# A fused attention, slot-mixture and feed-forward kernel: another buffer for the first head pair's maxima, and later places for the second and third pair's preparation

## The chip, the cores and the metric

The kernel runs on one core of one Trainium2 chip. The metric is the device time of one execution in microseconds (us), taken as the median of several runs.

## The reference, cut to what matters

Three stages follow one another. The change touches the first one alone.

```python
# attention: q, k, v are (4, 8, 1152, 64)
q_pool = q.reshape(B, H, S // 2, 2, D).mean(axis=3)      # 576 pooled queries
scores = matmul(q_pool, k.T) / sqrt(D)                    # 576 x 1152 for each head
attn = exp(scores - max(scores, axis=-1)); attn /= sum(attn) + 1e-9
out = matmul(attn, v)
# then a mixture with 8 experts x 4 slots (softmax over tokens and over slots)
# then x @ w_in, a piecewise quadratic activation, @ w_out
```

## The kernel before, in words

The 32 heads are handled as 16 pairs, P = 0 to 15. The keys of a pair are split into a high and a low fp16 part, which lie side by side in `kn` (`prep_khi` on ScalarE, L265; `prep_klo` on VectorE, L273, or on GpSimd for P = 1, L271), and are transposed by DMA into `K1[P]` (`xpose_k`, L279), one half of the tile for each head. The queries of a pair are added up in twos (`prep_qp`, L286), rounded to fp16 (`prep_qhi`, L289 and L291), transposed by DMA (`xpose_q1`, L301), and their remainder is kept in `qn2` (`prep_qlo`, L296). For P > 1 one more DMA copies the upper half of `q1[P]` into its lower half (`dup_q1`, L304). All loads, transposes and copies are issued by SyncE (SP), one after another.

A pair then has two jobs on TensorE. **Its maxima**: for each of nine query tiles t, `max_half(P, t, 0)` multiplies the queries by the difference of two halves of the keys (`KD`, written by `k_diff`, L315), ScalarE takes the positive part into `RW[:, t % 2]` (L332); `max_half(P, t, 1)` multiplies the queries by the first half, and VectorE adds and takes the running maximum (L335). `RW` has two places. The PSUM results take a tile of the pool `sc`, which has three buffers of two banks; two more banks, `acc0` and `acc1`, are the accumulators of the output. `max_fin(P)` turns the nine maxima into a row of the second query matrix `q2[P]`; for P = 0 this is done by TensorE (L354) and three evictions (L358 to L360), between two runs of filling products of the identity with itself (`fill`, L344). For P = 0 each `max_half(0, t, 0)` also issues two filling products (L330). **Its scores and output**: for each of nine key tiles c and each head h, `st` makes the scores (L383) and their exponential on ScalarE (L388, into a tile `e`), `pv` multiplies them by the values one step later (L408), and `es_add` sums the exponentials on VectorE (L394).

The order of the work is written out by hand. The steps are g = -11 to 144, two slots (h = 0, 1) in each; step g = 9 P + c does `st(P, c, h)`, `pv` of step g - 1, and the maxima of the pair that comes about one pair later. The first pair's maxima are at g = -11 to -3 with nothing beside them. The second pair's are at the steps that `P1G` lists, the third pair's start at g = 7. In a slot the order of issue is: maxima, `st`, `pv`, then what `sched` has for this slot, in the order in which `at` was called: `R1` (the second pair's preparation), the `k_diff` calls, and then pair by pair what `plan(P)` adds. `plan` turns a number x of `PREP` or `KDS` into the slot x % 2 of step 9 P + x // 2. Every engine and SP take their instructions in this order.

For P > 1 the loads go to buffers of which there is one: `kf` for keys, `qf` for queries, `kn` for the split keys. The pool hands a buffer to the next pair's tile only when everything that reads the tile before it is done, also a reader that stands later in the order; the engine that writes the new tile waits for it.

Of the kernel before, what the change touches and what calls it, by code (L numbers as in the profile page):

```python
# [12 lines left out]
AF = mybir.ActivationFunctionType  # L13
# [4 lines left out]


WARM = 8, 0, 4, 2, 6, 3, 3, 2  # L20
FILL = 38, 1, 6, 5

MB = {1: 3, 2: 10, 3: 20}
DU = (3, 4, 5)

CVS = (10, 12, 17, 18, 19), (8, 9, 10, 11, 12)
CVL = 1
P1G = 0, 1, 1, 2, 2, 3, 4, 5, 6
TML = (3, 0, 4), (6, 1, 4)
WPH = 6  # L30

# [2 lines left out]
       tuple((2 * c + h + 1 + (c < 8), c, h) for c in range(1, 9) for h in range(2)))  # L34
ADD += tuple((16, *x[1:]) if x == (17, 7, 0) else x for x in ADD[0]),

PREP = (-20, (-36, -35), (-34, -33), (-33, -32), -33, -32, -31, -30), (-24, (-42, -40), (-37, -37), (-35, -34), -38, -37, -35, -31)
KDS = -26, -19


@with_exitstack
def fused_kernel(ctx: ExitStack, tc: tile.TileContext, q, k, v, phi, w1, w2, w_in, w_out, out):
    nc = tc.nc
# [6 lines left out]
    HQ = TQ // 2  # L50
# [21 lines left out]
    def sc_tile(name):  # L72
        return sc_p.tile([128, 2, 512], F32, tag="sc", name=name)
# [95 lines left out]
    RW = g2.tile([128, 2, 2, HQ], F32, name="RW")  # L169
# [59 lines left out]
    K1, q1, q2, vt, qft, kft, qpt, mp = {}, {}, {}, {}, {}, {}, {}, {}  # L229
# [6 lines left out]
    def load_k(P, h):  # L236
        b, hp = divmod(P, HPB)
        if h == 0:

            kft[P] = g0.tile([128, 2, NK, D], F32, tag="kf", name=f"kf{P}") if P != 1 else \  # L240
                xT[:, 0:2].rearrange("p h (c d) -> p h c d", c=NK)
        nc.sync.dma_start(out=kft[P][:, h], in_=k[b, 2 * hp + h].rearrange("(p c) d -> p c d", p=128))
# [67 lines left out]
    def key_half(P, h):  # L310
        return K1[P][:, h * NK:(h + 1) * NK, :].rearrange("p c k -> p (c k)")
# [5 lines left out]
    def max_half(P, t, a):  # L317
        if t == 0 and a == 0:
            mp[P] = g2.tile([128, NK], F32, tag="mp", name=f"mp{P}")
        ps = sc_tile(f"mx{P}_{t}_{a}")  # L320
        parts = [(0, 64, 0 if t <= 4 else 1), (64, 128, 0 if t < 4 else 1)]
        for i in range(2):
            for (p0, p1, h) in parts:
                kk = key_half(P, h) if a else KD[:, h]
                nc.tensor.matmul(ps[p0:p1, i, 0:HQ], lhsT=q1[P][:, t, p0:p1], rhs=kk[:, i * HQ:(i + 1) * HQ],  # L325
                                 start=True, stop=True)
        if P == 0 and a == 0:
            for _ in range(FILL[1]):
                for p0 in (0, 64):
                    nc.tensor.matmul(fl[0][p0:p0 + 64, 0:HQ], lhsT=q1[P][:, t, p0:p0 + 64], rhs=kk[:, 0:HQ], start=True, stop=True)  # L330
        if a == 0:
            nc.scalar.activation(out=RW[:, t % 2], in_=ps[:, :, 0:HQ], func=AF.Relu)  # L332
        else:
            r = RW[:, t % 2]
            nc.vector.tensor_tensor_reduce(out=r, in0=ps[:, :, 0:HQ], in1=r, scale=1.0, scalar=-3.0e38, op0=ALU.add, op1=ALU.max,  # L335
                                           accum_out=mp[P][:, t:t + 1])

    fl = {}

    def fill(n):  # L340
        if not fl:
            fl[0] = acc_tile(0, "fill")
        for _ in range(n):
            nc.tensor.matmul(fl[0][:, 0:128], lhsT=ident, rhs=ident, start=True, stop=True)  # L344

    def max_fin(P):
        qn2 = qn2b[P % 2]
        nc.vector.tensor_scalar(out=qn2[:, :, D], in0=mp[P], scalar1=-1.0 / MS, scalar2=None, op0=ALU.mult)
        if P == 0:
            fill(FILL[2])  # L350
            ps = sc_tile("mr")
            po = [ps[64:96, 0], ps[64:96, 1], acc_tile(1, "mr8")[64:96]]
            for t in range(NK):
                nc.tensor.matmul(po[t // 4][:, t % 4 * 128:t % 4 * 128 + 128], lhsT=qn2[:, t, D:D + 1].to_broadcast([128, 32]),  # L354
                                 rhs=identh, start=True, stop=True)
            fill(FILL[3])
            f2 = q2[P].rearrange("p c k -> p (c k)")[64:96]
            nc.scalar.activation(out=f2[:, 0:512], in_=po[0], func=AF.Copy)  # L358
            nc.vector.tensor_copy(f2[:, 512:1024], po[1])
            nc.vector.tensor_copy(f2[:, 1024:1152], po[2][:, 0:128])  # L360
        else:
            xpose_q2(P)

    def xpose_q2(P):
        q2[P] = pr_p[P % 2].tile([128, NK, 128], F16, tag="q2", name=f"q2_{P}")
        nc.sync.dma_start_transpose(out=q2[P], in_=qn2b[P % 2].rearrange("p c k -> p (c k)"))
# [3 lines left out]
    def acc_tile(i, name):  # L370
        return acc_p.tile([128, 512], F32, tag=f"acc{i}", name=name)
# [192 lines left out]
    def at(g, slot, f, *a):  # L564
        sched.setdefault((g, slot), []).append((f, a))

    def plan(P):
        b = NK * P
        if P > 1:
            lk, hk, lok, xk, aq, hq_, xq, loq = PREP[P > 2]  # L570

            def sl(x, f, *a):
                at(b + x // 2, x % 2, f, *a)

            for h in range(2):
                at(b + lk, h, (load_k2, load_q)[h], P)
                sl(hk[h], prep_khi, P, h)
                sl(lok[h], prep_klo, P, h)
                sl(xk[h], xpose_k, P, h)
                sl(KDS[h], k_diff, P, h)  # L580
            sl(aq, prep_qp, P)
            sl(hq_, prep_qhi, P)
            sl(xq, xpose_q1, P)
            sl(loq, prep_qlo, P)
            sl(xq + (6 if P > 2 else 4), dup_q1, P)
        if P > 0:
            at(b - 8, 1, load_v, P)
            at(b - 4, 0, s2_fill, P, 0, 5)
            at(b, 0, s2_fill, P, 5, NK)
        last = P == NP - 1  # L590
        for s, *a in ADD[2 if P in (5, 9, 13) else last]:
            at(b + s // 2, s % 2, es_add, P, *a)
        if not last:
            pre.setdefault((b + 9, 0), []).append((es_sum, P))
        q_ = P // HPB
        if last:
            at(b + 9, 0, t_raw, P, 0)
            at(b + 9, 1, t_raw, P, 1)
            for f, *a in ((es_sum, P), (t_sum, P, 0), (t_sum, P, 1), (t_fin, P), (t_x, P, True), (warm, WARM[0]), (t_last, P),
                          (lg_mx, q_), (lg_tr, q_), (warm, WARM[5]), (lg_max, q_), (lg_rep, q_), (p_old, q_), (warm, WARM[1]), (lg_exp, q_),  # L600
                          (p_mm, q_), (warm, WARM[6]), (p_add, q_)):
                at(b + 10, 0, f, *a)
            return
        g0 = b + (11 if P == NP - 2 else 18)
        pre.setdefault((g0, 0), []).insert(0, (t_x, P))
        for i in range(2):
            at(g0, 0, t_ev, P, i)
        at(b + 10, 0, t_fin, P)
        for c, h, t in TML:
            at(g0 + c // 2, c % 2, t_mul, P, h, t)  # L610
        at(g0 + 3, 1, lg_add, P)
        for h in range(2):
            at(b + 9, h, t_raw, P, h)
            at(b + 9, h, t_sum, P, h)
        if P % HPB == HPB - 1:
            for s, f, *a in ((10, lg_mx), (12, lg_tr), (12, lg_max), (14, lg_rep), (14, lg_exp), (16, p_mm), (16, p_add)):
                late.setdefault((g0 + s // 2, s % 2), []).append((f, (q_, *a)))

    def slot(g, i):
        for d in (sched, late):  # L620
# [2 lines left out]

    R1 = (((-10, 1), (prep_khi, 1, 0), (prep_klo, 1, 0), (xpose_k, 1, 0)),
          ((-8, 1), (prep_khi, 1, 1), (prep_klo, 1, 1), (prep_qp, 1)),
          ((-6, 1), (xpose_k, 1, 1)),
          ((-3, 0), (prep_qhi, 1), (xpose_q1, 1)))

    with tc.manual_schedule():
        load_k(0, 0)  # L630
# [3 lines left out]
        load_k(1, 1)  # L634
        fill(FILL[0])
        nc.vector.memset(S2[64:128], 0.0)
# [31 lines left out]
                at(g, i, *x)  # L668
        at(-9, 1, k_diff, 0, 1)
        at(-3, 1, k_diff, 1, 0)  # L670
        at(0, 0, k_diff, 1, 1)
        at(1, 1, prep_qlo, 1)
        at(CVL, 1, cv_load, 0)

# [6 lines left out]
        for P in range(NP):  # L681
            plan(P)
# [11 lines left out]
        for g in range(-LEAD, nsteps + 1):  # L694
            mx = [divmod(g + LEAD, NK)] if not NK <= g + LEAD < 2 * NK else []
            mx += [(1, t) for t in range(NK) if P1G[t] == g]
            P, c = divmod(g, NK)
# [53 lines left out]
        def over_slots(ps, src):  # L751
            for dc in range(4):
                nc.tensor.matmul(ps[:, dc * NS:(dc + 1) * NS], lhsT=src[:, dc * 128:(dc + 1) * 128], rhs=st4,
                                 start=True, stop=True)
            return ps[:, 0:4 * NS].rearrange("p (c k) -> p c k", c=4)

        ps = over_slots(sc_tile("sT")[:, 0, :], Prun)
# [429 lines left out]
```

## Time and profile before

| | |
|---|---|
| median of 3 runs | 702.65 us (702.56, 702.65, 704.59) |
| the profiled execution's own time | 703.25 us |
| its span, first to last instruction | 701.4 us |
| busy: TensorE, VectorE, ScalarE, GpSimd | 690.0, 556.4, 497.5, 139.4 us |
[...]
| attention, g = -11 to 144 | from 12.3 us to about 430 us |

The times in the views below count from the start of the span. A row of the timeline gives the start, the duration, the engine, the line, the operation, written and read tiles, shape, count, and in brackets how long the engine had been idle and what ended that. PE is TensorE, PEld its weight loads, DVE VectorE, ACT ScalarE, SPq the queue of DMAs that SP issues. A matmul's duration runs to its modelled end, so two matmuls that follow one another overlap in the rows; the distance of their starts is what one costs.

### The profile page before, as it was taken

How to read it: one execution, taken by the hardware profiler on the slowest of the kernel's cores; microseconds unless marked ns; L12 is line 12 of the kernel's file. 1: busy time of each engine (PE TensorE's matmuls, PEld its weight loads, DVE VectorE, ACT ScalarE, POOL GpSimd, SP SyncE). 2: the span in 40 equal slices, each digit the busy share in tenths (PEclk: the TensorE clock that was granted, in tenths of full speed). 3: DMA queues.
4: the chain of work that ended last, by engine and by line, in shares of the span. 5: the costliest groups of instructions: out<-in, count | busy, mean ns of one | idle time of the engine just before them, and what ended most of it. 6: DMA issues, size and time to landing. Idle time of an engine off the chain costs nothing.

```text
span 701.4 us, 18916 instructions
## 1 busy us (share of the span) xinstructions
PE 690.0 (98%) x7639; PEld 548.1 (78%) x7639; DVE 556.4 (79%) x1094; ACT 497.5 (71%) x884; POOL 139.4 (20%) x123
## 2 busy tenths in 40 slices
PE   8899999999999999999999999999999999999997
PEld 8678878887888887888887876348888888888886
DVE  5699999999899999999998867327678888796542
ACT  4688888788788887788886865118787686677640
POOL 5100110110110110110010020113444353345340
PEclk9999999999999999999999999999999999999999
DMA  9978789988888987987885567993002212200222
GB/s 210 232 159 217 166 214 232 229 174 237 206 171 243 228 165 215 227 173 212 227 202 162 166 220 279 413 383 111 1 31 91 71 50 76 77 30 1 90 90 91
DMA packets 133766, 118.70 MB, mean 169 GB/s; under 512 B 81392, under 2 KB 103920, under 8 KB 131632
## 3 DMA queue, kind: packets, MB, share of 16 engines
q1 hardware_dynamic: 133680, 117.50, 61.9%
q8 instruction: 60, 0.98, 0.6%
q14 instruction: 26, 0.21, 0.1%
HBM read 82.90 MB, written 8.91 MB: 131 GB/s over the span
## 4 chain that ended last, share of the span: by engine, by line
PE 91%; DVE 4%; DMA 2%; ACT 1%; issue 1%; SPq 0%; POOL 0%; DVEq 0%; POOLq 0%; ACTq 0%
PE po L1023 27%; PE st L383 20%; PE acc L408 19%; PE mx L325 10%; PE h L953 2%; PE acc L401 2%; PE h L766 2%; DVE RW L335 2%; PE fill L344 2%; PE ty L448 1%; DMA Wst<-cv_dr 1%; PE tx L442 1%; PE s2o L823 1%; PE pb L537 1%; DVE es L394 0%
## 5 line engine op out<-in xcount | busy, mean ns | idle before, releaser
L388 ACT ACTIVATE e<-st 128x576 f32<-128x576 f32 x288 | 187.5, 652 | 53.0 <-PE st L383 51.9
L408 PE MATMUL acc<-e,vf 128*64 128x288 f32 x1152 | 198.4, 406 | 0.2 <-ACT e L388 0.2
L394 DVE TENSOR_TENSOR es<-es,e 128x576 f32<-128x576 f32 x194 | 144.4, 758 | 5.7 <-ACT e L388 0.4
L383 PE MATMUL st<-q,K 128*64 128x288 f16 x1152 | 129.5, 287 | 2.0 <-ACT e L388 0.5
L383 PE MATMUL st<-q,S 128*64 128x288 f16 x1152 | 129.5, 286 | 0.0
L335 DVE CUSTOM_DVE_ANT_0 RW<-mx,RW 128x576 f32<-128x576 f32 x144 | 108.4, 755 | 23.8 <-ACT e L388 14.2
L325 PEld LDWEIGHTS <-q 128*64 128x64 f16 x1152 | 74.3, 110 | 55.6 <-issue 8.4
L1023 PE MATMUL po<-whi,ghi 128*128 128x512 f32 x280 | 109.3, 390 | 0.0
L1023 PE MATMUL po<-wlo,ghi 128*128 128x512 f32 x280 | 109.0, 389 | 0.0
L1023 PE MATMUL po<-whi,glo 128*128 128x512 f32 x280 | 108.6, 388 | 0.0
L992 POOL TENSOR_TENSOR glo<-r,ghi 128x1024 fp32r<-128x1024 f32 x34 | 81.9, 2408 | 112.6 <-DVE r L980 66.3
L332 ACT ACTIVATE RW<-mx 128x576 f32<-128x576 f32 x144 | 93.4, 650 | 14.2 <-PE mx L325 9.5
L408 PEld LDWEIGHTS acc<-e,vf 128*64 128x64 f32 x1152 | 84.2, 137 | 2.1 <-ACT e L388 1.2
L383 PEld LDWEIGHTS <-K 128*64 128x64 f16 x1152 | 75.8, 109 | 11.7 <-issue 7.8
L489 POOL TENSOR_TENSOR xl<-xl,ss 128x320 f32<-128x320 f32 x15 | 12.5, 830 | 363.3 <-DVE wst L214 192.4
L383 PEld LDWEIGHTS <-S 128*64 128x64 f16 x1152 | 76.3, 110 | 1.0
L1035 DVE TENSOR_TENSOR pa<-po,pa 128x512 f32<-128x512 f32 (+1 forms) x54 | 36.8, 682 | 38.5 <-PE po L1023 38.4
L325 PE MATMUL mx<-KD,q 128*64 128x288 f16 x576 | 62.4, 287 | 3.1 <-DMA q<-qn 1.4
L325 PE MATMUL mx<-K,q 128*64 128x288 f16 x576 | 62.7, 288 | 0.1
L1023 PEld LDWEIGHTS po<-whi,glo 128*128 128x128 f32 x280 | 52.6, 188 | 11.4 <-POOL glo L992 0.3
L1023 PEld LDWEIGHTS po<-whi,ghi 128*128 128x128 f32 x280 | 52.7, 188 | 10.4 <-issue 0.4
L1023 PEld LDWEIGHTS po<-wlo,ghi 128*128 128x128 f32 x280 | 52.7, 188 | 9.5
(205 smaller groups left out, 900.6 us busy)
## 6 DMA issues: line engine op xcount, KB each, us to landing
w<-in_moe_w_dram SPq DMA_DIRECT2D x76, 256.0 KB, 4.0
w<-in_moe_w_dram SPq DMA_DIRECT2D x12, 1024.0 KB, 10.8
vf<-in_v_dram SPq DMA_DIRECT2D x16, 576.0 KB, 5.9
kf<-in_k_dram SPq DMA_DIRECT2D x30, 288.0 KB, 6.9
f<-in_moe_w_in_dram SPq DMA_DIRECT2D x16, 512.0 KB, 5.2
f<-in_moe_w_out_dram SPq DMA_DIRECT2D x16, 512.0 KB, 3.5
qf<-in_q_dram SPq DMA_DIRECT2D x30, 256.0 KB, 7.7
out_dram<-pa SPq DMA_DIRECT2D x17, 256.0 KB, 2.0
```

The costliest lines, as they stand in the source:

```text
L325: nc.tensor.matmul(ps[p0:p1, i, 0:HQ], lhsT=q1[P][:, t, p0:p1], rhs=kk[:, i * HQ:(i + 1) * HQ], start=True, stop=True)
L332: nc.scalar.activation(out=RW[:, t % 2], in_=ps[:, :, 0:HQ], func=AF.Relu)
L335: nc.vector.tensor_tensor_reduce(out=r, in0=ps[:, :, 0:HQ], in1=r, scale=1.0, scalar=-3.0e38, op0=ALU.add, op1=ALU.max, accum_out=mp[P][:, ...
L344: nc.tensor.matmul(fl[0][:, 0:128], lhsT=ident, rhs=ident, start=True, stop=True)
L383: nc.tensor.matmul(ps[c0:c0 + 64, i, 0:HQ], lhsT=kk[:, ci, c0:c0 + 64], rhs=f[:, sl[i]], start=first, stop=not first)
L388: nc.scalar.activation(out=e, in_=ps[:, :, 0:HQ], func=AF.Exp, scale=ESC)
L394: nc.vector.tensor_tensor(out=Es[P, h], in0=E[P, 0, h] if c == 1 else Es[P, h], in1=E[P, c, h], op=ALU.add)
L401: nc.tensor.matmul(acc[P, h][32 * r:32 * r + 32, HQ:HQ + SW], lhsT=ones.to_broadcast([128, 32]), rhs=a, start=False, stop=False, skip_grou ...
L408: nc.tensor.matmul(acc[P, i][h * 64:(h + 1) * 64, 0:HQ], lhsT=vt[P][:, h, c, :], rhs=E[P, c, h][:, i, :], start=(c == 0), stop=(c == NK - ...
L992: nc.gpsimd.tensor_tensor(out=glo[k], in0=r, in1=ghi[k].bitcast(F32), op=ALU.subtract)
L1023: nc.tensor.matmul(ps, lhsT=a, rhs=b, start=st_, stop=sp)
L1035: nc.vector.tensor_tensor(out=t, in0=po, in1=t, op=ALU.add)
```

## The change

Six things are changed. In the first pair's maxima, the products of odd t with the key difference go to the two accumulator banks in place of a buffer of `sc`, and ScalarE evicts every such product as two instructions of 288 columns. The filling products beside these maxima are left out. The two large pieces of the first pair's maximum row take two buffers, where they shared one. The second pair's maxima start at g = 2, and its last half of the keys' difference is made there. The transpose of the second half of the second pair's keys is issued behind that of its queries. The third pair's preparation is put three slots later in every part except the loads, and the first half of its key difference two slots later.

```diff
--- before.py
+++ after.py
@@ -18,14 +18,14 @@
 
 
 WARM = 8, 0, 4, 2, 6, 3, 3, 2
-FILL = 38, 1, 6, 5
+FILL = 38, 6, 5
 
 MB = {1: 3, 2: 10, 3: 20}
 DU = (3, 4, 5)
 
 CVS = (10, 12, 17, 18, 19), (8, 9, 10, 11, 12)
 CVL = 1
-P1G = 0, 1, 1, 2, 2, 3, 4, 5, 6
+P1G = 2, 2, 3, 3, 4, 4, 5, 5, 6
 TML = (3, 0, 4), (6, 1, 4)
 WPH = 6
 
@@ -34,8 +34,8 @@
        tuple((2 * c + h + 1 + (c < 8), c, h) for c in range(1, 9) for h in range(2)))
 ADD += tuple((16, *x[1:]) if x == (17, 7, 0) else x for x in ADD[0]),
 
-PREP = (-20, (-36, -35), (-34, -33), (-33, -32), -33, -32, -31, -30), (-24, (-42, -40), (-37, -37), (-35, -34), -38, -37, -35, -31)
-KDS = -26, -19
+PREP = (-20, (-33, -32), (-31, -30), (-30, -29), -30, -29, -28, -27), (-24, (-42, -40), (-37, -37), (-35, -34), -38, -37, -35, -31)
+KDS = (-24, -19), (-26, -19)
 
 
 @with_exitstack
@@ -317,18 +317,21 @@
     def max_half(P, t, a):
         if t == 0 and a == 0:
             mp[P] = g2.tile([128, NK], F32, tag="mp", name=f"mp{P}")
-        ps = sc_tile(f"mx{P}_{t}_{a}")
+        if P == 0 and a == 0 and t % 2:
+            ps = [acc_tile(i, f"mx0_{t}_{i}") for i in range(2)]
+        else:
+            ps = sc_tile(f"mx{P}_{t}_{a}")
+            ps = [ps[:, i] for i in range(2)] if P == 0 and a == 0 else ps
         parts = [(0, 64, 0 if t <= 4 else 1), (64, 128, 0 if t < 4 else 1)]
         for i in range(2):
             for (p0, p1, h) in parts:
                 kk = key_half(P, h) if a else KD[:, h]
-                nc.tensor.matmul(ps[p0:p1, i, 0:HQ], lhsT=q1[P][:, t, p0:p1], rhs=kk[:, i * HQ:(i + 1) * HQ],
-                                 start=True, stop=True)
+                o = ps[i][p0:p1] if P == 0 and a == 0 else ps[p0:p1, i]
+                nc.tensor.matmul(o[:, 0:HQ], lhsT=q1[P][:, t, p0:p1], rhs=kk[:, i * HQ:(i + 1) * HQ], start=True, stop=True)
         if P == 0 and a == 0:
-            for _ in range(FILL[1]):
-                for p0 in (0, 64):
-                    nc.tensor.matmul(fl[0][p0:p0 + 64, 0:HQ], lhsT=q1[P][:, t, p0:p0 + 64], rhs=kk[:, 0:HQ], start=True, stop=True)
-        if a == 0:
+            for i in range(2):
+                nc.scalar.activation(out=RW[:, t % 2, i], in_=ps[i][:, 0:HQ], func=AF.Relu)
+        elif a == 0:
             nc.scalar.activation(out=RW[:, t % 2], in_=ps[:, :, 0:HQ], func=AF.Relu)
         else:
             r = RW[:, t % 2]
@@ -347,13 +350,13 @@
         qn2 = qn2b[P % 2]
         nc.vector.tensor_scalar(out=qn2[:, :, D], in0=mp[P], scalar1=-1.0 / MS, scalar2=None, op0=ALU.mult)
         if P == 0:
-            fill(FILL[2])
-            ps = sc_tile("mr")
-            po = [ps[64:96, 0], ps[64:96, 1], acc_tile(1, "mr8")[64:96]]
+            fl.clear()
+            fill(FILL[1])
+            po = [x[64:96] for x in (sc_tile("mr0")[:, 0], sc_tile("mr1")[:, 0], acc_tile(1, "mr8"))]
             for t in range(NK):
                 nc.tensor.matmul(po[t // 4][:, t % 4 * 128:t % 4 * 128 + 128], lhsT=qn2[:, t, D:D + 1].to_broadcast([128, 32]),
                                  rhs=identh, start=True, stop=True)
-            fill(FILL[3])
+            fill(FILL[2])
             f2 = q2[P].rearrange("p c k -> p (c k)")[64:96]
             nc.scalar.activation(out=f2[:, 0:512], in_=po[0], func=AF.Copy)
             nc.vector.tensor_copy(f2[:, 512:1024], po[1])
@@ -577,7 +580,7 @@
                 sl(hk[h], prep_khi, P, h)
                 sl(lok[h], prep_klo, P, h)
                 sl(xk[h], xpose_k, P, h)
-                sl(KDS[h], k_diff, P, h)
+                sl(KDS[P > 2][h], k_diff, P, h)
             sl(aq, prep_qp, P)
             sl(hq_, prep_qhi, P)
             sl(xq, xpose_q1, P)
@@ -623,8 +626,7 @@
 
     R1 = (((-10, 1), (prep_khi, 1, 0), (prep_klo, 1, 0), (xpose_k, 1, 0)),
           ((-8, 1), (prep_khi, 1, 1), (prep_klo, 1, 1), (prep_qp, 1)),
-          ((-6, 1), (xpose_k, 1, 1)),
-          ((-3, 0), (prep_qhi, 1), (xpose_q1, 1)))
+          ((-3, 0), (prep_qhi, 1), (xpose_q1, 1), (xpose_k, 1, 1)))
 
     with tc.manual_schedule():
         load_k(0, 0)
@@ -668,7 +670,7 @@
                 at(g, i, *x)
         at(-9, 1, k_diff, 0, 1)
         at(-3, 1, k_diff, 1, 0)
-        at(0, 0, k_diff, 1, 1)
+        at(2, 0, k_diff, 1, 1)
         at(1, 1, prep_qlo, 1)
         at(CVL, 1, cv_load, 0)
 
```

By the rule for `PREP`, the third pair's parts stand here (step, slot), before and after: `prep_khi` (0,0) (0,1) and (1,1) (2,0); `prep_klo` (1,0) (1,1) and (2,1) (3,0); `xpose_k` (1,1) (2,0) and (3,0) (3,1); `prep_qp` (1,1) and (3,0); `prep_qhi` (2,0) and (3,1); `xpose_q1` (2,1) and (4,0); `prep_qlo` (3,0) and (4,1); `dup_q1` (4,1) and (6,0); the first `k_diff` (5,0) and (6,0). The fourth pair's loads stand at (3,0) for the keys and (3,1) for the queries in both kernels.

## Rows read from the trace of the kernel before

**Rows 1.** Page, the chain that ended last, by engine

```profile
PE 91%; DVE 4%; DMA 2%; ACT 1%; issue 1%; SPq 0%; POOL 0%; DVEq 0%; POOLq 0%; ACTq 0%
```

**Rows 2.** Timeline of PE, end of first pair's maxima

```profile
18.37 0.44 PE L325 MATMUL mx<-KD,q 128*64 128x288 f16 x4 [0.36 <-DVE mp L335]
...
21.08 1.60 PE L344 MATMUL fill<-ident 128*128 128x128 f32 x12
...
23.22 1.38 PE L344 MATMUL fill<-ident 128*128 128x128 f32 x10
26.02 0.44 PE L325 MATMUL mx<-KD,q 128*64 128x288 f16 x4 [1.42 <-DMA q<-qn]
26.29 0.41 PE L383 MATMUL st<-q,K 128*64 128x288 f16 x4
```

**Rows 3.** Groups by line, 12.2 to 24.8 us; columns: busy, mean ns, idle

```profile
L335 DVE CUSTOM_DVE_ANT_0 RW<-mx,RW 128x576 f32<-128x576 f32 x9 | 6.6, 756 | 2.3 <-ACT RW L332 1.2 <-PE mx L325 1.0
```

**Rows 4.** Timeline of ACT

```profile
27.04 0.65 ACT L388 ACTIVATE e<-st 128x576 f32<-128x576 f32 x1
27.57 0.69 ACT L265 ACTIVATE kn<-kf 128x576 f16<-128x576 f32 x1
...
53.37 0.41 ACT L419 ACTIVATE xT<-acc 128x288 f32<-128x288 f32 x1 [0.38 <-PE acc L401]
53.68 0.39 ACT L427 ACTIVATE es<-acc,cols 128x160 f32<-128x160 f32 x1
```

**Rows 5.** Timeline of DVE

```profile
13.44 0.76 DVE L335 CUSTOM_DVE_ANT_0 RW<-mx,RW 128x576 f32<-128x576 f32 x1 [0.40 <-ACT RW L332]
...
21.50 0.76 DVE L335 CUSTOM_DVE_ANT_0 RW<-mx,RW 128x576 f32<-128x576 f32 x1 [0.51 <-ACT RW L332]
...
23.89 0.69 DVE L359 CAST q<-mr 32x512 f16<-32x512 f32 x1 [1.34 <-ACT q L358]
...
36.60 0.76 DVE L394 TENSOR_TENSOR es<-es,e 128x576 f32<-128x576 f32 x1
37.27 0.75 DVE L296 SCALAR_TENSOR_TENSOR qn<-qf,qn 128x576 f16<-128x576 f32 x1
```

**Rows 6.** Timeline of PE, a step with one maximum

```profile
47.31 0.41 PE L325 MATMUL mx<-K,q 128*64 128x288 f16 x4
...
48.53 0.41 PE L325 MATMUL mx<-KD,q 128*64 128x288 f16 x4
```

**Rows 7.** Timeline of SP, the DMA issues

```profile
22.63 1.28 SPq L301 DMA_TRANSPOSE q<-qn  x1
...
35.66 1.98 SPq L301 DMA_TRANSPOSE q<-qn  x1
...
38.84 0.38 SPq L250 DMA_DIRECT2D qf<-in_q_dram  x1
...
40.38 0.59 SPq L253 DMA_DIRECT2D qf<-in_q_dram  x1
41.07 0.54 SPq L304 DMA_DIRECT2D q<-q  x1
...
43.53 0.61 SPq L308 DMA_DIRECT2D S<-K  x1
```

**Rows 8.** Timeline of PEld, start of third pair's maxima

```profile
46.06 0.14 PEld L325 LDWEIGHTS <-q 128*64 128x64 f16 x4 [0.55 <-DMA q<-q]
```

**Rows 9.** DMA issues, 36 to 48 us; last column: median us to landing

```profile
S<-K SPq DMA_DIRECT2D x1, 160.0 KB, 3.0
q<-q SPq DMA_DIRECT2D x1, 144.0 KB, 4.9
...
q<-qn SPq DMA_TRANSPOSE x2, 3.3
```

**Rows 10.** Two early stretches: busy us (count), PE first; then PEclk

```profile
4.00:6.00 2.00, 2.00 (x12) 2.00 (x10) 0.79 (x1) 0.33 (x1) 1.51 (x4) 1.00 1.01 265
...
8.00:10.00 2.00, 2.00 (x20) 2.00 (x20) 0.83 (x2) 0.53 (x1) 0.85 (x1) 1.00 0.99 127
```

## The prediction

> **What bounds the kernel now.** The page's chain comes first: nine tenths of the path that ends last are TensorE's own work [rows 1]. An edit in the attention therefore pays only where TensorE stands still, or if it takes products off TensorE, and what TensorE gains or loses in the first 46 us reaches the end one to one, since a later step with one maximum runs at TensorE's own pace, 48.53 - 47.31 = 1.22 us for a half step [rows 6]. So the next view is TensorE's timeline around the first pair's maxima. The reader is to see in it that fillings stand on both sides of the maximum row (21.08, 23.22), that the second of them ends at 24.60, and that TensorE then stands for 1.42 us until the transpose of the second pair's queries, issued at 22.63, is there [rows 2, 7]. The third view, VectorE's, shows the first pair's maxima themselves: the first running maximum starts at 13.44, the ninth at 21.50, so 1.01 us for each, while one takes 0.76 [rows 3, 5]. The fourth, the issues of SP beside TensorE's weight loads, shows where this stretch ends: at 46.06 the third pair's first maxima have waited for the DMA that copies its queries (L304), issued at 41.07 [rows 7, 8]. That place decides this prediction.
>
> **The change, part by part.**
>
> *First maxima.* With four buffers TensorE no longer waits for an eviction in every second tile, but `RW` keeps two places, so tile t + 2 must still follow tile t: running maximum 0.76, then ScalarE's positive part in two pieces, then the next. A piece of 288 columns takes 0.41, and the instruction behind it starts 0.31 after it [rows 4]; 0.76 + 0.31 + 0.41 and an estimated 0.08 for two handovers make 1.56 for two tiles, 0.78 for one. Eight tiles save 8 x (1.01 - 0.78) = 1.8; from this I take off 0.4, because two key conversions on ScalarE and one key difference on VectorE stand in the same queues: 1.4 us. Bounds: 1.0 if the two pieces do not overlap (0.82 in place of 0.72 for each tile), 2.1 if VectorE alone sets the pace (0.67 for an operation [rows 5]). The products left out cost nothing on the path, as TensorE has to wait there anyway. The splitting adds 2 x 0.31 - 0.53 = 0.09 to ScalarE for a tile [rows 4], inside that sum.
> [...]
>
> *Maximum row in two buffers.* VectorE's piece waited 1.34 us for ScalarE's [rows 5]; now they run side by side. The filling until 24.60 covers it; without that cover it would be 0.2.
>
> *Second pair's maxima at g = 2.* TensorE goes from the filling straight to the scores: not 26.29 [rows 2] but 24.60 - 1.4 = 23.2, a lead of 3.1 us. Left out for good is nothing; the nine tiles are pressed into g = 2 to 6, two in each of the first four.
>
> *Steps 0 to 6.* Steps 0 and 1 need the exponentials of the step before, so they end at about 26.7. From there VectorE sets the pace. Ahead of the second pair's first running maximum it has a key difference and two sums, which wait for the exponential of step 1 (26.9) and for the key transpose, now issued third, at about 22.6: first running maximum at 28.3 to 29.1, taken as 28.7. ScalarE's conversion of the third pair's keys, at 27.57 before [rows 4], waits for that transpose and those loads and fits the same bounds. From there to the third pair's `prep_qlo`, which now stands at slot (4,1), I count in the order of issue: six running maxima, four sums, two `prep_klo`, one `prep_qp`, `prep_qlo` itself: 14 operations of 0.67 to 0.68 [rows 5], 9.5 us, and one gap of 0.35, where the double step's products come later than VectorE is free. `prep_qlo` ends at X = 38.55 (37.8 to 39.1). Before, it ended at 37.27 + 0.75 = 38.02 [rows 5]. TensorE waits for VectorE's evictions until then: behind `prep_qlo` come a sum and the two running maxima of step 5, out at X + 3 x 0.68 = 40.6, and the scores, output and last maximum of step 6 take two half steps less the first product: TensorE is through at about 42.9, 3.2 earlier than 46.06.
>
> *SP's queue.* Here the lead is lost. The load of the fourth pair's queries stands at (3,1). Its buffer is the one from which `prep_qlo` reads, now at (4,1); before, that reader stood at (3,0), ahead of the load. So SP now stands at (3,1) until X. Queued behind it are the transpose of the third pair's queries at (4,0), two table loads, a copy of keys, and at (6,0) `dup_q1`. Before, that transpose was out at 35.66, ahead of the load [rows 7]. The four loads of queries take 40.38 + 0.59 - 38.84 = 2.13 to issue [rows 7], so the transpose goes out at X + 2.25. It lands 3.3 later by its own row [rows 9]; with the four loads just ahead of it I take 3.9, X + 6.15. The copy can't be issued before that. It took 4.9 with those loads ahead of it, and the like copy of keys 3.0 [rows 9]; the loads are through by now, so 3.0 is nearest: X + 9.15. Below, X + 8.6: the transpose and the three issues behind it occupy SP until X + 2.25 + 1.28 + (43.53 + 0.61 - 41.61) = X + 6.1 at best [rows 7], less a copy half a microsecond quicker. Above, X + 11.05, with a copy of 4.9. The third pair's first maxima start at 38.55 + 9.15 = 47.7 in place of 46.06: 1.6 us later. TensorE stands from 42.9 to 47.7, and the scores of step 7 stand behind the waiting maxima.
>
> *Behind it.* The second pair's transpose of `q2` is issued behind the copy, at about 45, takes 3.3 as the other transposes do [rows 9] and is needed at g = 9, about 52: hidden. Later pairs have the old order.
>
> **The sum.** A lead of 3.2 at step 6 and a pause of 4.8: in sum +1.6 on the profiled execution's 703.25 (span 701.4 and 1.85 around it), 704.85; that execution lies 0.60 above the median of the runs, so in terms of the median 702.65 it is 704.25, given as 704.2. This mechanism's own range is 702.4 (X = 37.8 and X + 8.6: +0.3, less 0.6 that backlogs of VectorE, worked off in the pause, may give back) to 706.2 (X + 11.05: +3.5).
>
> **The rivals.**
>
> *The clock falls in the pause (slower).* [...] What a start from rest costs is in the first 10 us: 12 filling products in 2 us, later 20 in 2 us, though the column says 1.00 in both [rows 10]. If that lasts 4 us (my estimate: at the start it is over by 8.00 at the latest), 16 of 40 products are missing, 1.6 us. Then +3.2: 705.9. For it: a pause three times as long as any that was survived. Against: no row shows a pause from which the clock fell. It decides if the pause is well over 1.42.
> [...]
>
> *SP isn't held (faster).* If the load of the fourth pair's queries doesn't wait for `prep_qlo`, the transpose is out before 35, the copy at about 39, and step 7 follows step 6 at 42.9: -3.2, 699.5. For it: everything on TensorE and VectorE gives the lead, and in the trace of before the wait never shows by itself, since SP came to this load only at 38.84, after 38.02 [rows 5, 7]. Against: the order of issue in `plan`, and one buffer for `qf`.
>
> *The copy lands late.* Copies of this kind with loads ahead of them take 4.9 [rows 9]; then X + 11.05 and 706.2, the forecast's mechanism at its upper end.
>
> **How the numbers follow.** A measurement of this kernel tells 0.3% from no change, 2.1 us: below 700.5 is faster, above 704.75 slower. The queue as forecast 0.58, the clock's fall 0.20, SP not held 0.17, anything else 0.05. Of the forecast's 0.58 about 0.17 lies above 704.75. Faster: 0.17 and a share of the rest, 0.19. Slower: 0.20 + 0.17 + 0.02 = 0.39. Same: 0.42. The range goes from 700.0, which takes in part of the faster case, to 706.4, which takes in the clock's case and the late copy.
>
> **What would show it.** SP's issue of the fourth pair's queries (L250) directly behind the end of the third pair's `prep_qlo`, the transpose L301 about 2.3 later; TensorE's wait at the third pair's first maxima put down to the DMA of L304, several us long; running maxima of the first pair at 0.78 each; the first scores near 23.2. A wait there of under 1 us, or L301 ahead of L250, would make the forecast wrong, and so would a first running maximum of the second pair well ahead of 28.3. A slow rate of products behind the pause would show the clock.

## The result and the profile after

The changed kernel takes 707.67 us (705.55 to 709.33, 6 runs), the kernel before 703.05 (702.54 to 704.67, 6 runs beside it): a ratio of 1.0061, 95% interval 1.0039 to 1.0082. It is slower, by more than the 0.3% that a measurement tells from no change, and lies outside the range given. The profiled execution took 709.33, span 707.6. Its mean granted clock was 0.994 of full speed, where the profiled execution of the kernel before has 1.000. Over the six executions the time goes with this clock: 705.55 us at 1.000, 707.27 and 707.49 at 0.998, 707.86 at 0.996, 708.52 and 709.33 at 0.994.

The page of after, the chain that ended last and the clock by slices; DMA and VectorE have a larger part in it than in [rows 1]:

```profile
PEclk9989999999999999999999999999999999999999
...
PE 88%; DVE 5%; DMA 3%; issue 1%; ACT 1%; SPq 1%; POOL 0%; DVEq 0%; ACTq 0%; POOLq 0%
```

TensorE's timeline of after, from step 6 to step 9 (to be held against [rows 6, 8]); the first of the L330 rows is step 7:

```profile
43.82 0.68 PE L411 MATMUL acc<-e,vf 128*64 128x288 f32 x4
48.44 0.69 PE L330 MATMUL mx<-KD,q 128*64 128x288 f16 x4 [3.94 <-DMA q<-q]
...
50.84 0.69 PE L330 MATMUL mx<-K,q 128*64 128x288 f16 x4
...
53.24 0.69 PE L330 MATMUL mx<-KD,q 128*64 128x288 f16 x4
...
55.04 0.41 PE L330 MATMUL mx<-K,q 128*64 128x288 f16 x4
...
56.26 0.41 PE L330 MATMUL mx<-KD,q 128*64 128x288 f16 x4
```

TensorE stands for 3.94 us for the copy of the third pair's queries. Step 7 starts at 48.44, 2.38 behind the 46.06 of [rows 8]. Then two half steps take 2.40 each and a third 1.80, where [rows 6] have 1.22: 6.60 - 3 x 1.22 = 2.9 us more. The windows of after show why (columns as in [rows 10]; the granted clock is the third number from the end):

```profile
44.00:48.00 4.00, 0.50 (x5) 0.00 (x0) 2.63 (x7) 0.76 (x2) 0.00 (x0) 0.95 0.72 147
48.00:50.00 2.00, 1.56 (x14) 1.25 (x16) 0.00 (x0) 0.65 (x1) 0.00 (x0) 0.50 0.62 138
...
52.00:54.00 2.00, 2.00 (x18) 1.21 (x14) 1.79 (x4) 0.68 (x2) 0.00 (x0) 0.50 0.00 0
...
56.00:60.00 4.00, 4.00 (x68) 2.83 (x66) 3.97 (x9) 3.16 (x7) 0.00 (x0) 1.00 0.14 33
```

Behind the pause the granted clock is 0.50, and it is back at 1.00 by 56. So 2.4 us of lateness and 2.9 of clock make 5.3 of the 6.2 by which this execution's span is longer. Of the remaining 0.9 some 0.6 come at 125.53, where TensorE waits 0.51 for a later pair's copy, as it doesn't in the kernel before; the other 0.3 come behind the attention, and their cause is not known.

SP's issues of after (to be held against [rows 7]), with VectorE's `prep_qlo` of the third pair at 39.16 in the fence behind it:

```profile
39.98 0.38 SPq L250 DMA_DIRECT2D qf<-in_q_dram  x1
...
41.52 0.60 SPq L253 DMA_DIRECT2D qf<-in_q_dram  x1
42.16 1.39 SPq L301 DMA_TRANSPOSE q<-qn  x1
...
45.73 0.55 SPq L304 DMA_DIRECT2D q<-q  x1
```

VectorE's timeline of after (to be held against [rows 5]):

```profile
13.76 0.76 DVE L338 CUSTOM_DVE_ANT_0 RW<-mx,RW 128x576 f32<-128x576 f32 x1 [0.48 <-ACT RW L333]
...
15.54 0.76 DVE L338 CUSTOM_DVE_ANT_0 RW<-mx,RW 128x576 f32<-128x576 f32 x1 [0.33 <-ACT RW L333]
...
16.22 0.45 DVE L315 TENSOR_TENSOR KD<-K 128x576 f16<-128x576 f16 x1
...
17.91 0.76 DVE L338 CUSTOM_DVE_ANT_0 RW<-mx,RW 128x576 f32<-128x576 f32 x1 [0.56 <-ACT RW L333]
...
19.52 0.76 DVE L338 CUSTOM_DVE_ANT_0 RW<-mx,RW 128x576 f32<-128x576 f32 x1 [0.16 <-ACT RW L333]
...
21.12 0.76 DVE L338 CUSTOM_DVE_ANT_0 RW<-mx,RW 128x576 f32<-128x576 f32 x1 [0.16 <-ACT RW L333]
...
22.26 0.19 DVE L351 TENSOR_SCALAR qn<-mp 128x9 f16<-128x9 f32 x1 [0.37 <-DMA q<-qn]
...
30.04 0.76 DVE L338 CUSTOM_DVE_ANT_0 RW<-mx,RW 128x576 f32<-128x576 f32 x1 [0.98 <-ACT RW L335]
...
39.16 0.75 DVE L296 SCALAR_TENSOR_TENSOR qn<-qf,qn 128x576 f16<-128x576 f32 x1
```

`prep_qlo` ends at 39.16 + 0.75 = 39.91, and SP issues the load of the fourth pair's queries at 39.98: the load was held by the reader. The transpose follows 2.25 later and the copy goes out at 45.73. The first maxima end at 21.12 + 0.76, hardly earlier than the 21.50 + 0.76 of [rows 5].

The first maximum product starts at 11.8 to 12.9 us from one execution to another. Below, places are therefore also given from that product: step 7 is at 46.06 - 12.28 = 33.78 before and at 48.44 - 12.54 = 35.90 after.

### The profile page after: what moved, and what is told of

Its sections match the earlier page's. It is cut to its first block, busy times and chain, and to the rows that moved or that the text cites. A ratio compares the mean times of both kernels' runs of the same rounds, so it can differ in the third digit from the quotient of the medians.

```text
span 707.6 us, 18894 instructions
## 1 busy us (share of the span) xinstructions
PE 692.4 (98%) x7621; PEld 548.8 (78%) x7621; DVE 556.6 (79%) x1094; ACT 497.9 (70%) x893; POOL 139.9 (20%) x123
## 4 chain that ended last, share of the span: by engine, by line
PE 88%; DVE 5%; DMA 3%; issue 1%; ACT 1%; SPq 1%; POOL 0%; DVEq 0%; ACTq 0%; POOLq 0%
PE po L1025 27%; PE st L386 19%; PE acc L411 17%; PE mx L330 8%; PE h L955 2%; PE acc L404 2%; PE h L768 2%; PE s2o L825 2%; PE fill L347 2%; DVE RW L338 2%; DMA q<-q 2%; PE ty L451 1%; DVE es L397 1%; PE tx L445 1%; DMA q<-qn 1%
## 5 line engine op out<-in xcount | busy, mean ns | idle before, releaser
L330 PEld LDWEIGHTS <-q 128*64 128x64 f16 x1152 | 74.8, 110 | 59.1 <-issue 10.0
L335 ACT ACTIVATE RW<-mx 128x576 f32<-128x576 f32 x135 | 87.4, 650 | 10.1 <-PE mx L330 5.8
L330 PE MATMUL mx<-KD,q 128*64 128x288 f16 x576 | 63.1, 289 | 5.5 <-DMA q<-q 4.4
L330 PE MATMUL mx<-K,q 128*64 128x288 f16 x576 | 62.7, 289 | 1.1 <-DVE mp L338 0.7
```

The source lines that it names most:

```text
L330: nc.tensor.matmul(o[:, 0:HQ], lhsT=q1[P][:, t, p0:p1], rhs=kk[:, i * HQ:(i + 1) * HQ], start=True, stop=True)
```

## The experiments

Ratios are to the kernel before on the same chip, with the 95% interval. No experiment leaves out part of the computation.

### What the copy and the clock cost

**Fourth pair's load of queries behind the copy.** On the changed kernel:

```diff
-                at(b + lk, h, (load_k2, load_q)[h], P)
+                at(b + lk + (h if P == 3 else 0), h, (load_k2, load_q)[h], P)
-            sl(xq + (6 if P > 2 else 4), dup_q1, P)
+            sl(xq + (6 if P > 2 else 1), dup_q1, P)
```

> The changed kernel with two issues of SP moved: the copy of the third pair's queries at slot (4,1), right behind their transpose, and the load of the fourth pair's queries behind it, after the reader that it waits for. Everything else is as changed. Theory A (the pause at step 7 comes from SP standing in front of that load): the transpose goes out at about 37.1, where the last key transpose has left SP, lands at about 40.5, the copy lands at 43.5 to 45.4; TensorE is ready for step 7 at 44.3, so the pause is 0 to 1 us in place of 3.9, step 7 starts at 44.3 to 45.4 against 46.06 before the change and 48.44 after it, the granted clock stays at 1.00, and the time is 701.3 to 702.7. Rival B (the loss comes from nine tiles pressed into five steps and from evictions in two pieces): TensorE is held by VectorE all the same and the time stays above 704.5.

Measured: 703.78 us, ratio 1.0003 (0.9993 to 1.0012): slower than theory A had it, but under the 704.5 of rival B. Lines of this kernel's SP and TensorE timelines:

```profile
36.06 2.93 SPq L301 DMA_TRANSPOSE q<-qn  x1
42.57 0.49 SPq L304 DMA_DIRECT2D q<-q  x1
```

```profile
45.00 0.44 PE L330 MATMUL mx<-KD,q 128*64 128x288 f16 x4 [0.68 <-ACT e L391]
...
52.25 0.44 PE L386 MATMUL st<-q,S 128*64 128x288 f16 x4 [1.69 <-DMA q<-qn]
```

The transpose goes out 6.1 us earlier than after, the 3.94 us pause and with it the loss are gone. What the rest of the change gained is lost again in two places: the copy still goes out only at 42.57, 6.5 behind its transpose, and at step 9 TensorE stands 1.69 us for the second pair's `q2`, whose transpose now stands behind the four loads (issued at 47.62).

**The pause filled with products.** On the changed kernel, ahead of the third pair's first maxima; nothing reads them:

```diff
+        if P == 2 and t == 0 and a == 0:
+            hold = sc_tile("hold")
+            for _ in range(14):
+                nc.tensor.matmul(hold[:, 0, 0:128], lhsT=ident, rhs=ident, start=True, stop=True)
```

> The changed kernel with 14 products of the identity with itself, about 0.28 us each, in front of the third pair's first maxima, where TensorE waits for the copy; they write a buffer that nothing reads. The order of SP is not touched. Theory A1 (of the loss, some 2.4 us are the late copy, and the rest is TensorE's clock, which fell to 0.50 in the pause): step 7 starts at 48.2 to 48.8 as in the changed kernel, its half steps take 1.2 us at once in place of 2.4, the clock is 1.000 in every run, and the time is 705.0 to 705.8. Rival A2 (the slow half steps after the pause come from something that the pause doesn't cause): they stay at 2.4 us and the time stays at 707 to 709.

Measured: 706.10 us, ratio 1.0035 (1.0023 to 1.0047), 0.3 us above the time expected. Its TensorE timeline, and one of its windows:

```profile
44.83 3.39 PE L328 MATMUL hold<-ident 128*128 128x128 f32 x28
48.83 0.44 PE L334 MATMUL mx<-KD,q 128*64 128x288 f16 x4 [0.61 <-DMA q<-q]
...
50.08 0.41 PE L334 MATMUL mx<-K,q 128*64 128x288 f16 x4
```

```profile
48.00:50.00 2.00, 1.39 (x19) 1.00 (x19) 0.00 (x0) 0.69 (x2) 0.00 (x0) 1.00 0.76 167
```

Step 7 is as late as after (48.83 - 12.88 = 35.95 from the first product), but the granted clock stays at 1.00 and the half steps take 1.25 and 1.22 at once. This parts the two costs: 0.35% are left, 2.5 us, which go with the late copy (step 7 starts 2.17 later than before), and the clock is 0.0061 - 0.0035 of 703, 1.8 us in the medians (the intervals of the two ratios overlap a little; in the profiled execution the rows show 2.9). The one execution of the changed kernel at a mean clock of 1.000 gives the same 2.5: 705.55 - 703.05.

**The third pair's prep at its old place.** On the changed kernel:

```diff
-PREP = (-20, (-33, -32), (-31, -30), (-30, -29), -30, -29, -28, -27), ...
-KDS = (-24, -19), (-26, -19)
+PREP = (-20, (-36, -35), (-34, -33), (-33, -32), -33, -32, -31, -30), ...
+KDS = (-26, -19), (-26, -19)
```

> The changed kernel with the third pair's preparation and first key difference where they were before; fourth buffer, no filling products, second pair's maxima from g = 2 and the later key transpose stay. Theory A: the load of the fourth pair's queries stands behind its reader again, the copy is out by about 42 and step 7 has no long pause; in exchange ScalarE waits in step 0 for the second pair's last key transpose (landed at about 26.9 in the changed kernel) before it can write the third pair's split keys, which costs TensorE 0.5 to 1.5 us in steps 0 and 1. Step 7 at 43.5 to 46, time 700.5 to 703, clock 1.00. Rival B (the pressed maxima): above 704.5, as this keeps them.

Measured: 706.75 us, ratio 1.0044 (1.0032 to 1.0056): missed. Its timelines of ScalarE and TensorE, and a window:

```profile
27.81 0.68 ACT L265 ACTIVATE kn<-kf 128x576 f16<-128x576 f32 x1 [2.71 <-DMA kf<-in_k_dram]
28.40 0.63 ACT L391 ACTIVATE e<-st 128x576 f32<-128x576 f32 x1
```

```profile
29.09 0.74 PE L411 MATMUL acc<-e,vf 128*64 128x288 f32 x1 [3.21 <-ACT e L391]
```

```profile
30.00:32.00 2.00, 2.00 (x15) 1.53 (x12) 0.83 (x3) 0.92 (x2) 0.00 (x0) 0.50 0.91 238
```

The held queue is gone, but now ScalarE stands at the third pair's key conversion for a load that hasn't landed, the exponential of step 1 stands behind it, TensorE behind that for 3.21 us, and the clock falls again. Two parts of the change work together here, and no run separates them: with the second pair's maxima moved to g = 2, step 1 comes earlier, and the load of the third pair's keys goes out later, 2.77 us behind the transpose of the second pair's queries (24.57 - 21.80), where it was 1.33 before (23.96 - 22.63), since a transpose of keys now stands between them. So the later places of the prep were needed, and it is the load of the fourth pair's queries that ought to have moved along.

**`prep_qlo` late, alone.** On the kernel before:

```diff
-PREP = (-20, (-36, -35), (-34, -33), (-33, -32), -33, -32, -31, -30), ...
+PREP = (-20, (-36, -35), (-34, -33), (-33, -32), -33, -32, -31, -27), ...
```

> The kernel before with one edit: the third pair's prep_qlo at slot (4,1), its place in the changed kernel, with all else (the transpose of its queries at (2,1), the loads at (3,0) and (3,1)) as before. Theory of the held queue: SP stands at the load of the fourth pair's queries until prep_qlo is through, at about 41; the copy L304 goes out about 2.1 later and lands 3.0 to 4.9 behind that, so step 7 starts at 46.3 to 48.2 in place of 46.06 and the time rises by 0.3 to 2.2 us, ratio 1.0004 to 1.0031, with the load's issue right behind prep_qlo's end. If the queue does not stand there, the load goes out at 38.8 as before and the ratio is 1.0 within 0.0005.

Measured: 704.18 us, ratio 1.0010 (1.0001 to 1.0019). One line each of its VectorE and TensorE timelines, two of SP's:

```profile
41.73 0.75 DVE L296 SCALAR_TENSOR_TENSOR qn<-qf,qn 128x576 f16<-128x576 f32 x1
```

```profile
42.51 0.38 SPq L250 DMA_DIRECT2D qf<-in_q_dram  x1
...
44.73 0.54 SPq L304 DMA_DIRECT2D q<-q  x1
```

```profile
47.24 0.44 PE L325 MATMUL mx<-KD,q 128*64 128x288 f16 x4 [0.61 <-DMA q<-q]
```

`prep_qlo` ends at 42.48, the load is out at 42.51, the copy 2.2 later: one late reader of a buffer holds SP, in a kernel where nothing else differs. Here the transpose had gone out before, so only the copy stands behind the load, and it costs 0.6 us in the medians; in the profiled executions step 7 starts 0.78 later from the first product (47.24 - 12.68 = 34.56 against 33.78).

**Both loads of the fourth pair at slot (4,1).** On the changed kernel, with `dup_q1` at `xq + 1` as in the first experiment:

```diff
+                at(*((4, 1) if P == 3 else (b + lk, h)), (load_k2, load_q)[h], P)
```

> As the run with the mended queue, but both loads of the fourth pair, keys and queries, are issued at slot (4,1) behind the copy of the third pair's queries, so that the rings hold neither when the transpose and the copy go out. Theory A (order of SP and the transfers ahead in the rings set step 7): the transpose is out at about 35.8, lands in 3.5 to 4.5 in place of 6.4, the copy lands by 43; step 7 starts 31.5 to 32.5 us after the first product of the first maxima (33.8 before the change, 35.9 after it, 32.7 with the mended queue). The second pair's last transpose (its second query matrix) then has the two loads ahead of it, with 2 us more to go than in the mended queue, and step 9 waits less than 1 us for it (1.7 there). Time 701.2 to 702.8. Rival: the stretch is bound by the transfers as a whole, so what the copy gains the later transpose loses: step 9 waits 2 us or more and the time is 703.3 or more.

Measured: 702.26 us, ratio 0.9982 (0.9973 to 0.9991): faster than both kernels by the interval, though less than 0.3% faster than the kernel before. Its SP and TensorE timelines:

```profile
36.62 1.32 SPq L301 DMA_TRANSPOSE q<-qn  x1
40.19 0.49 SPq L304 DMA_DIRECT2D q<-q  x1
...
41.91 0.38 SPq L250 DMA_DIRECT2D qf<-in_q_dram  x1
```

```profile
44.12 0.44 PE L330 MATMUL mx<-KD,q 128*64 128x288 f16 x4
```

Without the load of keys ahead of it, the copy goes out 3.6 behind its transpose (6.5 in the first experiment). Step 7 waits for nothing at 44.12 - 12.23 = 31.89, 1.9 earlier than before.

**The same loads in the kernel before.** The edit of the line above, on the kernel before, and nothing else:

> The kernel before with one edit: both loads of the fourth pair (keys and queries) stand at slot (4,1), behind the third pair's copy of queries, as in the run with the loads behind the copy; nothing else of the change is in it. Theory: that run's gain needs the lead of the changed maxima, and here the copy was only 0.55 us late, so at most 0.5 us is to be had: 0.9992 to 1.0, step 7 at 45.5 to 46.06. Rival: the place of the loads alone makes the gain, then 0.9982 as in that run, 1.2 us.

Measured: 702.91 us, ratio 0.9993 (0.9984 to 1.0002). The copy is out at 39.08 (41.07 in [rows 7]), nothing waits for it, and step 7 is at 45.21 - 11.77 = 33.44, 0.34 earlier than before. So the place of the loads alone gives about half a microsecond, as the theory has it, and the interval doesn't exclude nothing at all; that the 1.2 us of the run above need the changed maxima as well is likely, but not shown, as the intervals of the two overlap.

### Where the gain of the first maxima stayed

**First maxima alone.** On the kernel before, only the edits to `max_half`, `max_fin` and `FILL`.

> The kernel before with the first pair's maxima as changed (fourth buffer, evictions in two pieces, no filling products beside them, maximum row in two buffers) and nothing else of the change. My account: the ninth running maximum starts 0.4 us earlier than in the kernel before (21.12 against 21.50 in the changed kernel), since in place of the buffer TensorE waits for the second key difference, and the maximum row has to wait for a transpose that still reads its tile; step 0 still waits for the transpose of the second pair's queries. Time 702.4 to 703.2, no change that can be told; clock 1.00. If the evictions in two pieces or the missing products did harm by themselves, it would be above 704.

Measured: 703.44 us, ratio 1.0000 (0.9989 to 1.0011). The conversion (L351) starts 21.25 - 11.80 = 9.45 behind the first product, against 10.08 before and 9.72 after. TensorE then still waits 1.38 us for the transpose of [rows 2].

**Second key difference earlier.** On that kernel:

```diff
-        at(-9, 1, k_diff, 0, 1)
+        at(-10, 1, k_diff, 0, 1)
```

> The run with the first maxima alone, with the second half of the first pair's key difference one step earlier (behind the second running maximum, not the third), so that TensorE doesn't wait 0.9 us for it. Theory A (a floor: the conversion of the nine maxima writes a tile that the transpose of the first pair's query remainder still reads, and that lands 6.2 to 6.7 us after its issue at about 15.4): the ninth running maximum starts 0.4 to 0.9 earlier, but the conversion starts at 21.6 to 22.2 as before, waiting for that DMA, and the time is that of the run it is based on, 703 to 703.8. Rival B (the second difference was what limited the fourth buffer): the conversion moves by the same 0.4 to 0.9, and the time falls to 702.4 to 703.

Measured: 703.26 us, ratio 0.9991 (0.9981 to 1.0001), conversion at 9.62. The ninth running maximum starts 20.61 - 11.86 = 8.75 behind the first product, against 8.58 in the run it is based on: no gain where both theories had one. Its timelines of VectorE, GpSimd and TensorE, and a window:

```profile
14.44 1.45 DVE L315 TENSOR_TENSOR KD<-K 128x576 f16<-128x576 f16 x1
```

```profile
14.30 1.28 POOL L271 TENSOR_TENSOR kn<-xT,kn 128x576 f16<-128x576 f32 x1 [0.85 <-ACT kn L265]
```

```profile
47.80 0.44 PE L330 MATMUL mx<-KD,q 128*64 128x288 f16 x4 [2.60 <-DMA q<-q]
```

```profile
48.00:50.00 2.00, 2.00 (x30) 1.61 (x28) 0.39 (x1) 1.72 (x4) 0.00 (x0) 1.00 0.52 117
```

The difference was issued earlier, but takes 1.45 us where it took 0.45 after: it has run into GpSimd's remainder of the keys (14.30 to 15.58). The last two lines are by the way: in this execution the copy landed 5.3 us after its issue, and behind a pause of 2.60 the clock stood at 1.00.

**Maximum row in a tile of its own**, so that the conversion needn't wait for the transpose that reads `qn2`. On the kernel above:

```diff
+    mq = cst([128, NK], "mq", F16)
-        nc.vector.tensor_scalar(out=qn2[:, :, D], in0=mp[P], ...)
+        nc.vector.tensor_scalar(out=qn2[:, :, D] if P else mq, in0=mp[P], ...)
```

The products of the maximum row then read `mq` too.

> The run before this, with the first pair's nine converted maxima in a small tile of their own, so that their conversion waits for no transpose. Theory A: the conversion starts 8.4 to 9.1 us after the first product of the maxima (10.1 in the kernel before, 9.7 in the changed one), the second pair's queries go out that much earlier, and the time falls by 0.5 to 1.2 against the kernel before: 702.2 to 702.9. Rival B: nothing moves, as step 0 waits for the second pair's transpose whenever it is issued, since the rings are full: 703 to 703.8.

Measured: 703.07 us, ratio 1.0000 (0.9986 to 1.0014), conversion at 9.56. The wait of 0.37 in after was no standing cost: in the run before this, which still has the old tile, the conversion starts 0.11 us behind the end of the ninth running maximum (21.37, 21.48).

**All of it together**, on the run with both loads behind the copy:

> The changed kernel with all of these: both loads of the fourth pair behind the copy, the second key difference one step earlier, the maxima's row in a tile of its own. If both theories A hold: step 7 starts 30.8 to 32 us after the first product, no pause of TensorE over 1 us up to step 9, clock 1.00, time 700.4 to 702.2, faster than the kernel before. If the transfers bind the stretch as a whole, the lead is lost at step 7 or at step 9 again: 703 or more.

Measured: 702.72 us, ratio 0.9991 (0.9981 to 1.0001). Step 7 is at 43.73 - 11.75 = 31.98, no earlier than with the loads alone; the difference takes 1.45 here too.

**The key difference without GpSimd beside it.** On two of the kernels above, the one with the second key difference earlier and the one with all of it together, the preparation of the first half of the second pair's keys two slots later:

```diff
-    R1 = (((-10, 1), (prep_khi, 1, 0), (prep_klo, 1, 0), (xpose_k, 1, 0)),
+    R1 = (((-9, 1), (prep_khi, 1, 0), (prep_klo, 1, 0), (xpose_k, 1, 0)),
```

> On the run with the second difference early: the preparation of the first half of the second pair's keys two slots later, at (-9,1), so that GpSimd's instruction for it no longer stands beside the second key difference on VectorE. In that run the difference took 1.45 us beside a GpSimd instruction from 14.30 to 15.58, where it takes 0.45 elsewhere. Theory: the two exclude each other, and this ate what the earlier place would give; now the difference takes 0.45 to 0.5 and the conversion of the maxima starts 8.6 to 8.9 us behind the first product in place of 9.62. Rival: the long duration has another cause (its operand, the keys' transpose), then it stays at 1.45 and 9.6. The whole time is expected at 0.999 to 1.0, as the third pair's copy still sets the end of this stretch.

> The same move on the run with all mended parts (loads behind the copy, second difference early, own tile for the row). Theory: the conversion starts 8.6 to 8.9 us behind the first product, and as no DMA is waited for at step 7 there, up to 0.8 of it reaches the end: 701.9 to 702.5, ratio 0.998 to 0.9988. Rival: VectorE's work ahead of step 7 takes it back, then it stays at 0.9991.

Measured: 703.31 us, ratio 0.9989 (0.9981 to 0.9998), and for all parts together 702.61 us, ratio 0.9973 (0.9962 to 0.9985). VectorE and GpSimd of the first of them:

```profile
15.06 0.45 DVE L315 TENSOR_TENSOR KD<-K 128x576 f16<-128x576 f16 x1
...
16.48 0.76 DVE L338 CUSTOM_DVE_ANT_0 RW<-mx,RW 128x576 f32<-128x576 f32 x1 [0.29 <-ACT RW L333]
...
17.65 0.76 DVE L338 CUSTOM_DVE_ANT_0 RW<-mx,RW 128x576 f32<-128x576 f32 x1 [0.41 <-ACT RW L333]
```

```profile
15.93 2.52 POOL L271 TENSOR_TENSOR kn<-xT,kn 128x576 f16<-128x576 f32 x2 [3.26 <-ACT kn L265]
```

With GpSimd out of the way the difference takes 0.45 again, so the collision is the cause. The conversion starts at 9.25 and 9.18, not at the 8.6 to 8.9 expected: the next two running maxima now wait for ScalarE (0.29, 0.41), which has the key conversions in the same queue. Together with the later loads this is the fastest ratio to the kernel before; against the loads alone (0.9982) the intervals don't tell the two apart.

## Why the prediction was wrong

**The held queue: right.** The load came out directly behind `prep_qlo` (39.91, 39.98), the transpose 2.25 behind that as worked out, and the copy was what step 7 waited for. X itself was 39.91, outside the 37.8 to 39.1 given; from there step 7 started after 8.53, a tenth below the 8.6 to 11.05 (9.15 taken). The experiments confirm it in both directions: with the load moved the loss is gone, and `prep_qlo` alone brings the hold into the kernel before.

**The clock: the failing step.** The text gave "the clock falls in the pause" a chance of 0.20 and a price of 1.6 us. It fell, by the mean clock in five of the six executions. The condition that the text named, a pause well over the 1.42 of [rows 2], behind which the clock stood at 1.00, was its own forecast of 4.8 (3.94 came), and so the rival hung on an event that was already expected; only the absence of a row of such a fall spoke against it, which is no evidence that it doesn't happen. In the profiled execution the price was 2.9, since the clock stayed low over two and a half half steps; 1.8 in the medians. That 1.8 lies near the 1.6 is luck: the 1.6 was taken from 4 us at the rate of the kernel's start, and in the profiled execution the rows behind the pause show 6 us at half the clock.

The clock alone would not have carried the time out of the range: 704.2 + 1.8 = 706.0, under 706.4. Of the 0.61%, 4.3 us, the forecast had 1.6; 1.8 are the clock, which its sum put at nothing, and the remaining 0.9 go for the most part with a step 7 that came 0.74 later than forecast (48.44 against 47.7), because the next term was too large as well.

The trace of after has the row that was missing: 0.50 granted from 48 to 54, behind a wait of 3.94 for a DMA.

**First maxima: mis-sized.** 1.4 us were forecast (bounds 1.0 to 2.1; with the 0.67 that it names, and the same 0.4 taken off, the upper one comes out at 2.3); from before to after it is 24.60 - 24.42 = 0.2, and 0.4 from the first product. The pace itself came out: two tiles in 1.61 and 1.60 (17.91, 19.52, 21.12) against 1.56 worked out; the 0.08 for two handovers in it was an estimate that no row shows, and beside 0.76 + 0.31 + 0.41 the measured pace leaves 0.12 to 0.13 for them. But only the later tiles reach it, and over all eight it is 0.92 for each. Two tiles take 1.78 at the start (13.76 to 15.54), and the next two 2.37, around the second key difference: the 0.4 taken off for key conversions and key difference was 1.0. The transpose of the queries' remainder held the conversion for another 0.37 in this execution. The bound of 1.0 "if the two pieces do not overlap" was no bound for what stood in the same queues.

**ScalarE's two pieces: right.** Two pieces of 288 took 0.71 us in after's row of two, at 20.38, against 0.72 in the sum.

**Steps 0 to 6: the distance right, the start late.** From the second pair's first running maximum to the end of `prep_qlo` I worked out 9.85; it is 39.91 - 30.04 = 9.87. But that maximum started at 30.04, not 28.7 (28.3 to 29.1): the first scores, which were to start at 23.2, started at 24.42, 1.2 later, which is the missing gain of the first maxima. So X came 1.4 later, and step 7 at 48.44 in place of 47.7. TensorE was through step 6 at 44.50 (42.9 forecast).

**The rivals.** "SP isn't held" was wrong as argued. "The copy lands late" did not happen in after (2.7 us from issue to landing), though it did in the run with the second key difference early, at 5.3.

## What to carry to other kernels

When a reader of a single-buffered tile is moved later, move the load of its next tile along, or everything behind that load in the DMA queue is held; here that cost 2.5 us, without the clock, where the transpose and copy of the next stage stood behind it. A forecast pause of TensorE that is longer than any in the trace must carry the clock in its main line, not as a rival: here a pause of 3.94 was followed by 0.50 granted, 1.8 us in the medians. Products that nobody reads, put into that pause, kept the clock at 1.00 and left the 2.5 us of the late copy. Before taking waits out of a chain, list what else stands in the queue of the engine that sets its pace, and what another engine does beside it: the key difference took 1.45 us in place of 0.45 beside GpSimd.

## What was not expected of the hardware

**VectorE's key difference took three times as long beside GpSimd.** The fp16 key difference took 0.45 us with no GpSimd instruction beside it (15.06, the key difference without GpSimd beside it) and 1.45 beside GpSimd's 1.28 us subtraction (14.44 and 14.30, second key difference earlier), and ended 0.3 behind it; in after it lay, by its place in the order, just between two of them. A running maximum, which reads PSUM and one tile of SBUF, took 0.74 beside the next such subtraction (16.49 beside 16.07 to 17.35, second key difference earlier). The first pair's `prep_qlo`, which reads two tiles of SBUF as the key difference does, shows both beside GpSimd's multiplication of a tile by a scalar: in the kernel before it took 0.74 from 11.82 (multiplication L653 from 10.92, 1.66 long), in after 1.22 from 11.58 (L655 from 11.28, 1.91 long). What sets the two apart, these rows don't show.

**Length of the pause and clock.** Behind pauses of 1.42 [rows 2] and 2.60 us (second key difference earlier) the granted clock stood at 1.00; behind pauses of 3.21 (third pair's prep at its old place) and 3.94 (after) it stood at 0.50 for some 6 us more, which cost about 2.9 in the latter. These are single cases, and no rule follows from them: the changed kernel has such a pause in its order of work, and one of its six executions ran at a mean clock of 1.000.

**The landing time of one copy.** The third pair's copy `q<-q` of 144 KB landed 2.3 to 5.3 us after its issue in the nine runs whose landing is at hand. It took 4.9, 3.7 and 5.3 in the three (the kernel before, third pair's prep at its old place, second key difference earlier) where the fourth pair's keys (two loads of 288 KB) had gone out 3.4 to 4.1 us before it, and 2.3 to 2.8 in the six others. The four loads of queries, to which the prediction put the 4.9, are not enough: in the run with `prep_qlo` late, alone, they stand directly ahead of the copy, the keys 6.95 before it, and it took 2.5. Where the copy stood directly behind its transpose on SP, it was let out 3.3 us (the last kernel, all parts together) to 6.5 us (first experiment, a load of keys ahead of the transpose) after the transpose was issued.
